# Second batch's first stage over eight slots at two groups each, three quarters of its copies on VectorE

## Chip, cores, metric

One core of one Trainium2 chip. The metric is the device time of one execution in microseconds (us), median of the runs given. The granted clock is the share of TensorE's full clock that the profile shows as let through. Engines: TensorE (PE, its weight loads PEld), VectorE (DVE), ScalarE (ACT), GpSimd (POOL).

## The reference, cut

```python
# x: (8, 3008, 256) fp32; filt_r, filt_i: (1505, 256); w_in: (256, 2048); w_out: (2048, 256)
X = np.fft.rfft(x, axis=1)
y = np.fft.irfft(X * (filt_r + 1j * filt_i)[None], n=3008, axis=1)      # filter along the sequence
h = y.reshape(24064, 256) @ w_in
out = np.maximum(0.01 * h, h) @ w_out                                   # leaky ReLU between two products
```

## The kernel before: the parts that matter

The Fourier transform of each batch is done in stages by matrix products: a first stage (`s1`, 16 groups of two matmuls), transposes (`t1`), spectral products (`s2`, `sa`, 12 groups each), transposes (`t2`), an inverse stage (`sb`, 16 groups). The feed-forward part ("moe") runs in chunks of 512 tokens. After batch 0, everything is laid out in slots: each slot has one feed-forward group of four matmuls, the Fourier tasks of a later batch, and, from slot 8 on, eight matmuls of the second product.

```python
wide   = [psp.tile([P, 2 * CH], FP32, name=f"ph{i}") for i in range(2)]   # two double banks: feed-forward
single = [psp.tile([P, CH], FP32, name=f"pf{i}") for i in range(3)]       # three single banks: Fourier stages
# ...
def s1_group(b, g, copy=nc.scalar.copy):
    def go():
        ps = bank("pf", 2, D)
        for j in range(2):
            n2 = 2 * g + j
            nc.tensor.matmul(ps[:, j, :], f1_sb[:N1, n2, :], x_sb[:N1, n2, :], start=True, stop=True)
        spread(big[(4 * b) % 3], 2 * g, ps, copy)          # the copy out of the bank: L187 in the profile
    return go
# ...
def plan(b, s1, per, t1, s2, step, lag, t2, sb):
    for g in range(16):
        at(s1 + g // per, s1_group(b, g, dve if b == 1 and g % 2 else act))
    if b + 1 < B:
        at(s1 + 15 // per, lambda: x_load(b + 1))
    for i in range(4):
        at(t1 + i, t1_part(b, i))
    for g in range(12):
        at(s2 + (step * g) // 4, s2_group(b, g))
        at(s2 + lag + (step * g) // 4, sa_group(b, g))
    for i in range(4):
        at(t2 + i, t2_part(b, i))
    for g in range(16):
        at(sb + g // 2, sb_group(b, g, dve))               # inverse, copied out by VectorE: L246

# batch, first slot of s1, its groups a slot, first slot of t1, of s2,
# slots per four groups of s2, lag of sa behind s2, first slot of t2, of sb
plan(1, 0, 3, 6, 12, 4, 3, 26, 31)
for b in range(2, B):
    z = 47 * (b - 1) - 8
    plan(b, z, 2, z + 9, z + 13, 5, 3, z + 32, z + 37)

for slot in range(SL * (NCHUNK + 1)):
    ci, g = divmod(slot, SL)
    if ci < NCHUNK:
        moe1_group(ci, g)              # matmuls L376, then the activation on ScalarE, L381
    for f in tasks.get(slot, ()):
        f()
    if ci > 0:
        moe2_slice(ci - 1, g)          # matmuls L390; every second slot ScalarE copies the result out, L397
```

Of the kernel before, what the change touches and what calls it, by code (L numbers as in the profile page):

```python
# [65 lines left out]
def kernel(  # L66
# [50 lines left out]
    def bank(kind, n, w):  # L117
        of = wide if kind == "ph" else single
        t = of[turn[kind] % len(of)]
        turn[kind] += 1  # L120
        return t[:, : n * w].rearrange("p (n w) -> p n w", n=n)
# [7 lines left out]
    def x_load(b, n0=0, nn=N2, d0=0, dn=D):  # L129

        for lo, cnt in ((0, R1),) if b + 1 < B else ((0, 64), (64, N1 - 64)):
            nc.gpsimd.dma_start(  # L132
                x_sb[lo : lo + cnt, ds(n0, nn), ds(d0, dn)],
                bass.AP(tensor=x.tensor, offset=x.offset + (b * N + lo * N2 + n0) * D + d0,
                        ap=[[N2 * D, cnt], [D, nn], [1, dn]]))
# [35 lines left out]
# [5 lines that stand above are left out]
                nc.tensor.matmul(ps[:, j, :], f1_sb[:N1, n2, :], x_sb[:N1, n2, :],  # L176
                                 start=True, stop=True)
            spread(big[(4 * b) % 3], 2 * g, ps, copy)
        return go
# [5 lines left out]
    def spread(dst, n0, ps, copy, e0=0):  # L185
        nn, de = ps.shape[1], ps.shape[2] // 2
        copy(paired(dst)[:, ds(n0, nn), ds(e0, de)], ps.rearrange("p n (e t) -> p n e t", t=2))  # L187
# [3 lines left out]
    def t1_part(b, i, flat=False):  # L191
        def go():
            a = big[(4 * b) % 3][:].bitcast(FP32)[:, ts(i, E4 * Q)].rearrange("p (e n) -> p e n", n=Q)
            o = big[(4 * b + 1) % 3][:].bitcast(FP32)
            if flat:
                o = o[:, ts(i, E4 * Q)].rearrange("p (e n) -> p e n", n=Q)
            else:
                o = o.rearrange("p (n e) -> p e n", n=Q)[:, ts(i, E4), :]
            nc.vector.transpose(o, a)  # L199
        return go  # L200


    def t2_part(b, i):
        def go():
            a = big[(4 * b + 2) % 3][:].bitcast(FP32)[:, ts(i, E4 * Q)].rearrange("p (e n) -> p e n", n=Q)
            o = big[(4 * b + 3) % 3][:].bitcast(FP32).rearrange("p (h n e) -> p h e n", h=2, n=Q)
            nc.vector.transpose(o[:, i // 2, ts(i % 2, E4), :], a)  # L207
        return go
# [3 lines left out]
    def s2_group(b, g):  # L212
        def go():
            ps = bank("pf", 2, D)
            src = big[(4 * b + 1) % 3][:].rearrange("p (n d) -> p n d", n=Q)
            nc.tensor.matmul(ps, fwd2, src[:, ds(2 * g, 2), :], start=True, stop=True)  # L216
            fa, fb = fa_sb[:, ds(2 * g, 2), :], fb_sb[:, ds(2 * g, 2), :]
            p1 = scrp.tile([P, 2, D], FP32, tag="p1", name=f"p1_b{b}_g{g}")
            p2 = scrp.tile([P, 2, D], FP32, tag="p2", name=f"p2_b{b}_g{g}")
            nc.vector.tensor_tensor(p1[:], ps, fa, AL.mult)  # L220
            nc.vector.tensor_tensor(p2[0:64], ps[64:P], fb[64:P], AL.mult)  # L221
            nc.vector.tensor_tensor(p2[64:P], ps[0:64], fb[0:64], AL.mult)  # L222
            y1 = ypp.tile([P, 2, D], FP16, tag="y", name=f"y_b{b}_g{g}")
            nc.gpsimd.tensor_tensor(y1[:], p1[:], p2[:], AL.add)  # L224
            ys[(b, g)] = y1
        return go

    def sa_group(b, g):
        def go():
            ps = bank("pf", 2, D)  # L230
            nc.tensor.matmul(ps, inv2, ys.pop((b, g))[:], start=True, stop=True)  # L231
            spread(big[(4 * b + 2) % 3], 2 * g, ps, nc.scalar.copy)
        return go

    def sb_group(b, g, copy):
        dt, h = g // 8, g % 8

        def go():
            src = big[(4 * b + 3) % 3][:].rearrange("p (h n d) -> p h n d", h=2, n=Q)
            ps = bank("pf", 4, N1)  # L240
            for j in range(4):
                n2 = 4 * h + j
                nc.tensor.matmul(ps[:, j, :], src[:, dt, n2, :], i1_sb[:, n2, :],  # L243
                                 start=True, stop=True)
            yv = yts[b % 2][:, dt, :].rearrange("p (a c) -> p a c", c=N2)
            copy(yv[:, :, ds(4 * h, 4)], ps.rearrange("p c a -> p a c"))  # L246
        return go
# [3 lines left out]
    act, dve = nc.scalar.copy, nc.vector.tensor_copy  # L251
# [70 lines left out]
    g = 0  # L322
    for n0, nn in first_parts:
        while nn:
            n = 2 if nn % 4 or n0 >= N2 - 4 else 4
            first_s1(n0, n, two[n // 4], (dve, act)[g % 2])
            n0, nn, g = n0 + n, nn - n, g + 1
# [79 lines left out]
    def at(slot, f):  # L407
        tasks.setdefault(slot, []).append(f)

    def plan(b, s1, per, t1, s2, step, lag, t2, sb):  # L410
        for g in range(16):
            at(s1 + g // per, s1_group(b, g, dve if b == 1 and g % 2 else act))
        if b + 1 < B:
            at(s1 + 15 // per, lambda: x_load(b + 1))
        for i in range(4):
# [6 lines that stand above are left out]
        for g in range(16):  # L422
            at(sb + g // 2, sb_group(b, g, dve))

    plan(1, 0, 3, 6, 12, 4, 3, 26, 31)
    for b in range(2, B):
        z = 47 * (b - 1) - 8
        plan(b, z, 2, z + 9, z + 13, 5, 3, z + 32, z + 37)

    for slot in range(SL * (NCHUNK + 1)):  # L430
        ci, g = divmod(slot, SL)
# [36 lines left out]
```

## Time and profile before

| | before |
|---|---|
| time, first three runs | 783.71 us (783.41 to 784.31) |
| span of the trace, granted clock | 783.3 us, 1.000 |
| TensorE / ScalarE / VectorE busy | 99% / 71% / 47% |
| first first-stage matmul of batch 1 | 43.85 us |
| from there to slot 8's feed-forward group | 10.96 us |
| from slot 8's group to the start of the last 64 matmuls of the second product (one line of the timeline) | 717.81 us |

Matmul records overlap: a group of four is recorded with 1.03 us and the next matmul starts 0.87 us after it began, because the profile models the end. So all TensorE intervals here are from start to start. The two ends of the 10.96 us in the timeline, batch 1's first first-stage matmul and the group that follows slot 8's feed-forward group (which starts at 54.81, 0.86 us earlier):

```profile
43.85 0.82 PE L176 MATMUL pf<-x_sb,f_sb 94*128 94x256 f16 x6
...
55.67 1.04 PE L390 MATMUL po_ps<-w_out_sb,gt_c 128*128 128x256 f16 x8
```

### The profile page before, as it was taken

The page shows a single profiled execution, that of the slowest core. Times are in us where ns is not written, and L with a number is a line of the kernel's source. Part 1 is how long each engine was busy: PE and PEld are TensorE (multiplying, and loading weights), DVE is VectorE, ACT ScalarE, POOL GpSimd, SP SyncE. Part 2 cuts the span into 40 slices and gives each one's busy share as a digit, 9 for nine tenths or more (in the row PEclk, how much of TensorE's full clock was granted, in tenths as well). Part 3 has the DMA queues.
Part 4 walks back from the last instruction along what each step waited for, and adds up shares of the span by engine and source line. Part 5 has one row for each costly group of instructions (what it writes and reads, how often), then busy time and mean ns, then how long its engine had stood idle before and what let it go on. Part 6 is the DMA issues. An engine that isn't in the chain of part 4 may idle for free.

```text
span 783.3 us, 13680 instructions
## 1 busy us (share of the span) xinstructions
PE 773.6 (99%) x5844; PEld 531.3 (68%) x5844; DVE 364.6 (47%) x458; ACT 553.2 (71%) x788; POOL 151.7 (19%) x126
## 2 busy tenths in 40 slices
PE   8899999999999999999999999999999999999998
PEld 4356677666776677766777667776677666676666
DVE  3868751875237641477306754088432765200000
ACT  3686759776686767777687775967768776666664
POOL 5974300250003300052001510025000340000000
PEclk9999999999999999999999999999999999999999
DMA  9972102301041101510105101140101001101111
GB/s 174 228 115 67 41 28 51 98 28 42 28 95 55 41 28 41 107 40 30 42 28 113 36 29 40 42 107 28 41 28 41 29 28 41 41 31 37 41 41 55
DMA packets 39388, 44.17 MB, mean 56 GB/s; under 512 B 11266, under 2 KB 37506, under 8 KB 38658
## 3 DMA queue, kind: packets, MB, share of 16 engines
q0 software_dynamic: 13136, 17.78, 13.3%
q1 hardware_dynamic: 26192, 25.53, 9.3%
q8 instruction: 45, 0.74, 0.4%
q14 instruction: 15, 0.12, 0.1%
HBM read 35.67 MB, written 24.64 MB: 77 GB/s over the span
## 4 chain that ended last, share of the span: by engine, by line
PE 93%; ACT 2%; DMA 1%; issue 1%; POOL 1%; DVE 1%; ACTq 0%; POOLq 0%
PE po_ps L390 41%; PE ph L376 41%; PE pf L176 3%; PE pf L243 2%; PE pf L216 2%; PE pf L231 2%; DMA x_sb<-in_x_dram 1%; ACT big L187 1%; PE pf L390 1%; POOL fy_h_c L276 1%; ACT gt_c L381 1%; PE ph L265 0%; PE po_ps L318 0%; DVE big L297 0%; DVE big L199 0%
## 5 line engine op out<-in xcount | busy, mean ns | idle before, releaser
L381 ACT ACTIVATE gt_c<-ph 128x1024 f16<-128x1024 f32 x376 | 385.1, 1025 | 194.6 <-PE ph L376 193.6
L376 PE MATMUL ph<-yt,w_in_sb 128*128 128x512 f16 (+7 forms) x1728 | 386.6, 351 | 0.4 <-ACT gt_c L381 0.2
L390 PE MATMUL po_ps<-w_out_sb,gt_c 128*128 128x256 f16 x2944 | 381.4, 272 | 0.6 <-ACT ost_c_t L397 0.6
L390 PEld LDWEIGHTS <-gt_c 128*128 128x128 f16 x3008 | 290.7, 98 | 86.7 <-issue 1.7
L376 PEld LDWEIGHTS <-w_in_sb 128*128 128x128 f16 x1728 | 163.0, 98 | 95.2 <-issue 1.1
L224 POOL TENSOR_TENSOR y_b_g<-p_b_g,p_b_g 128x512 f16<-128x512 f32 x84 | 106.9, 1273 | 225.8 <-DVE p_b_g L222 225.8
L199 DVE STREAM_TRANSPOSE big<-big 128x1024 f32<-128x1024 f32 x32 | 55.8, 1844 | 127.1 <-ACT big L187 127.0
L187 ACT CAST big<-pf 128x512 f16<-128x512 f32 x190 | 108.9, 605 | 2.2 <-PE pf L256 2.2
L246 DVE CAST yt<-pf 128x376 f16<-128x376 f32 x112 | 56.3, 544 | 85.9 <-PE pf L243 85.9
L220 DVE TENSOR_TENSOR p_b_g<-pf,fa_sb 128x512 f32<-128x512 f32 x84 | 58.1, 692 | 38.9 <-PE pf L216 36.3
L397 ACT COPY ost_c_t<-po_ps 128x256 f32<-128x256 f32 x184 | 69.3, 377 | 6.6 <-PE po_ps L390 5.5
L207 DVE STREAM_TRANSPOSE big<-big 128x1024 f32<-128x1024 f32 x28 | 51.1, 1940 | 34.1 <-ACT big L187 34.1
L221 DVE TENSOR_TENSOR p_b_g<-pf,fb_sb 64x512 f32<-64x512 f32 x84 | 58.2, 692 | 1.1
L222 DVE TENSOR_TENSOR p_b_g<-pf,fb_sb 64x512 f32<-64x512 f32 x84 | 57.4, 683 | 1.1
L132 POOL DMA_DIRECT2D x_sb<-in_x_dram x12 | 6.6, 553 | 253.8 <-PE pf L176 253.0
L243 PEld LDWEIGHTS <-big 128*128 128x128 f16 x448 | 25.6, 98 | 13.2
L176 PE MATMUL pf<-x_sb,f_sb 94*128 94x256 f16 x224 | 33.8, 272 | 0.1
L216 PE MATMUL pf<-big,small_sb 128*128 128x512 f16 x84 | 31.8, 379 | 0.0
L231 PE MATMUL pf<-y_b_g,small_sb 128*128 128x512 f16 x84 | 31.8, 379 | 0.0
L243 PE MATMUL pf<-i_sb,big 128*128 128x94 f16 x448 | 28.7, 206 | 0.0
L176 PEld LDWEIGHTS <-f_sb 94*128 94x128 f16 x224 | 21.0, 97 | 9.5 <-issue 1.3
L318 PE MATMUL po_ps<-idle 128*128 128x512 f16 x72 | 18.9, 406 | 1.2 <-DVE one L165 1.2
(46 smaller groups left out, 155.3 us busy)
## 6 DMA issues: line engine op xcount, KB each, us to landing
out_dram<-ost_c_t SPq DMA_DIRECT2D x92, 256.0 KB, 2.1
x_sb<-in_x_dram POOLq DMA_DIRECT2D x6, 1536.0 KB, 10.9
x_sb<-in_x_dram POOLq DMA_DIRECT2D x3, 480.0 KB, 9.8
fa_sb<-in_filt_r_dram POOLq DMA_DIRECT2D x6, 192.0 KB, 10.0
fb_sb<-in_filt_i_dram POOLq DMA_DIRECT2D x6, 192.0 KB, 8.5
w_in_sb<-in_moe_w_in_dram POOLq DMA_DIRECT2D x1, 1024.0 KB, 13.0
w_out_sb<-in_moe_w_out_dram POOLq DMA_DIRECT2D x1, 1024.0 KB, 12.7
x_sb<-in_x_dram POOLq DMA_DIRECT2D x1, 1024.0 KB, 8.1
```

What stands on the lines that cost most here:

```text
L176: nc.tensor.matmul(ps[:, j, :], f1_sb[:N1, n2, :], x_sb[:N1, n2, :], start=True, stop=True)
L187: copy(paired(dst)[:, ds(n0, nn), ds(e0, de)], ps.rearrange("p n (e t) -> p n e t", t=2))
L220: nc.vector.tensor_tensor(p1[:], ps, fa, AL.mult)
L221: nc.vector.tensor_tensor(p2[0:64], ps[64:P], fb[64:P], AL.mult)
L222: nc.vector.tensor_tensor(p2[64:P], ps[0:64], fb[0:64], AL.mult)
L224: nc.gpsimd.tensor_tensor(y1[:], p1[:], p2[:], AL.add)
L243: nc.tensor.matmul(ps[:, j, :], src[:, dt, n2, :], i1_sb[:, n2, :], start=True, stop=True)
L246: copy(yv[:, :, ds(4 * h, 4)], ps.rearrange("p c a -> p a c"))
L376: nc.tensor.matmul(ph[:, j, ds(o, ln)], w_in_sb[:, dt, ts(ct, P)], yts[b % 2][:, dt, ds(lo, ln)], start=(dt == 0), stop=(dt == NDT - 1),)
L381: nc.scalar.activation(gts[ci][:, ds(2 * g, 2), :], ph, AF.Lrelu)
L390: nc.tensor.matmul(po, gts[ci][:, ct, ts(tj, P)], w_out_sb[:, ct, :], start=(ct == 0), stop=(ct == NCT - 1))
L397: nc.scalar.copy(ost[:, tj % 2, :], po)
```

## The change

Intent: in slots 0 to 7 ScalarE has both the activations and half of the first-stage copies of batch 1. Spreading the groups and giving VectorE twelve of the sixteen copies should let TensorE set the pace. The later stages of batch 1 move by a slot.

```diff
-            at(s1 + g // per, s1_group(b, g, dve if b == 1 and g % 2 else act))
+            at(s1 + g // per, s1_group(b, g, dve if b == 1 and g % 4 < 3 else act))
...
-    plan(1, 0, 3, 6, 12, 4, 3, 26, 31)
+    plan(1, 0, 2, 8, 13, 4, 3, 27, 32)
```

## The prediction

> **What bounds the kernel now.** I read the page first (busy shares, then the chain that ended last), then the waits, then the timeline of the stretch that the change touches. The busy shares and the chain:
>
> ```profile
> PE 773.6 (99%) x5844; PEld 531.3 (68%) x5844; DVE 364.6 (47%) x458; ACT 553.2 (71%) x788; POOL 151.7 (19%) x126
> PE 93%; ACT 2%; DMA 1%; issue 1%; POOL 1%; DVE 1%; ACTq 0%; POOLq 0%
> ```
>
> TensorE is 93% of the chain. A busy TensorE can still hide gaps, so I checked the pace: from the start of one four-matmul group to the next instruction group the timeline shows 0.87 us (0.217 us for each 512 columns) and 0.44 us for four first-stage matmuls of 256 columns (0.11 us each), everywhere after 55 us. There the same work takes the same time however it is ordered, so no reordering gains anything. A gain can only come from a stretch where TensorE is not at that pace. The chain in order of time shows where the other engines enter it:
>
> ```profile
> 42.60 0.56 DVE yt L309
> 45.94 1.05 ACT gt_c L381
> ...
> 49.33 1.07 ACT gt_c L381
> ...
> 51.74 1.15 ACT big L187 x2
> 52.89 0.94 ACT gt_c L381
> ...
> 53.87 1.97 PE ph L376 x8
> ```
>
> From 44 to 53.9 us the chain runs through ScalarE; then TensorE takes it over. This is exactly slots 0 to 7 of the second phase, where the second batch's first stage is packed three groups to a slot. The timeline of TensorE and ScalarE there, with durations whose modelled matmul ends overlap (so I use starts only):
>
> ```profile
> 48.03 1.03 PE L376 MATMUL ph<-yt,w_in_sb 128*128 128x512 f16 x4
> 48.32 1.16 ACT L187 CAST big<-pf 128x512 f16<-128x512 f32 x2
> 49.33 1.07 ACT L381 ACTIVATE gt_c<-ph 128x1024 f16<-128x1024 f32 x1
> 49.75 1.03 PE L376 MATMUL ph<-yt,w_in_sb 128*128 128x512 f16 x4
> 50.24 0.71 ACT L187 CAST big<-pf 128x512 f16<-128x512 f32 x1
> 51.44 1.03 PE L376 MATMUL ph<-yt,w_in_sb 128*128 128x512 f16 x4
> ...
> 52.67 1.03 PE L376 MATMUL ph<-yt,w_in_sb 128*128 128x512 f16 x4
> 53.87 1.97 PE L376 MATMUL ph<-yt,w_in_sb 128*128 128x512 f16 x8 [0.17 <-ACT gt_c L381]
> ```
>
> Two slots take 51.44 - 48.03 = 3.41 us. TensorE needs for them 2 x 0.87 + 6 x 0.22 = 3.06 us; ScalarE has two activations and three copies and is busy without a gap (10.71 us of the 10.96 between 43.85 and 54.81 by the windows view). So ScalarE paces the stretch, and TensorE loses about 0.17 us a slot, plus some at 52.7 to 53.9, where the last activations drain.
>
> The second place that matters is where batch 1 ends and batch 2 begins, at slots 38 and 39:
>
> ```profile
> 115.38 0.51 PE L243 MATMUL pf<-i_sb,big 128*128 128x94 f16 x8
> 115.74 1.03 PE L390 MATMUL po_ps<-w_out_sb,gt_c 128*128 128x256 f16 x8
> 115.76 1.01 DVE L246 CAST yt<-pf 128x376 f16<-128x376 f32 x2 [1.08 <-PE pf L243]
> 116.61 1.03 PE L376 MATMUL ph<-yt,w_in_sb 128*128 128x512 f16 x4
> 117.47 0.60 PE L176 MATMUL pf<-x_sb,f_sb 94*128 94x256 f16 x4
> ```
>
> The last inverse groups (L243) run in slot 38, VectorE takes their banks from 115.76 to 116.77, and batch 2's first stage (L176) starts a slot later, after its banks are free. Nothing waits.
>
> [...] VectorE's copies record 0.69 us and follow one another at 0.60, ScalarE's record 0.605 in the mean, and the activation 1.025. So moving a copy to VectorE makes it a little slower, not free. [...] Here the first stage, the spectral stages and the inverse all rotate through the same three single banks, and the activations' matmuls through two double ones. [...] the matmul at 53.87 starts 0.04 us after the activation that emptied its bank.
>
> **The change, part by part.** Nothing is removed; all counts of matmuls, copies and transfers stay.
>
> 1. *Sixteen groups over eight slots at two each.* TensorE then needs 0.87 + 0.44 = 1.30 us a slot.
> 2. *Twelve of sixteen copies on VectorE (eight before).* ScalarE has, per two slots, two activations and one copy. At the spacing seen (an activation and the next start 0.92 apart, a copy 0.55) that is about 2 x 0.95 + 0.55 = 2.45 us against 2.61 for TensorE. VectorE has three copies: 3 x 0.65 = 1.95 us. So TensorE becomes the slowest, by 0.16 us per two slots.
> 3. *Do the bank rotations keep up?* A double bank is filled in 0.87, picked up 0.2 us later, held 1.02 and released: about 2.1 us after its first matmul, and needed again 2.61 after it. Where a copy sits ahead of the activation on ScalarE the margin falls to about 0.25 us. A single bank is needed again three groups later, 1.5 slots or 1.52 us at the nearest; a VectorE copy of the second group of a slot, queued behind the first, is done about 1.55 us after its matmuls start against 2.4 needed in that phase. All margins are positive but none is large.
> 4. *The sum for the first stretch.* The first activation group still waits for the yt copy ending at 43.15, so the first stage still starts at 43.85. Between there and the ninth group (start of slot 8) lie 7 x 0.867 + 16 x 0.218 = 9.56 us at full pace, so slot 8 starts at 53.41. Before, the x8 entry at 53.87 holds two groups; the second, slot 8's, starts 54.81 in the trace (the next group follows at 55.67). Gain: 54.81 - 53.41 = 1.40 us.
> 5. *The later stages move by one slot.* The transposes need all sixteen copies; the last is now ScalarE's, behind slot 7's activation, done at about 52.1 + 2.6 = 54.7. The four take 7.28 us (53.74 to 61.02 before), so end near 62.0. The first spectral matmul stands in slot 13, at 53.41 + 5 x 1.735 + 0.87 = 62.95. It has 0.9 us to spare. The other intervals (5 slots from transpose to spectral, 14 to the second transpose, 5 to the inverse) are as before or shorter by that one slot, and the input load that follows the first stage has over 40 us before it is read. No cost.
> 6. *The new collision.* Batch 1's inverse now ends in slot 39, where batch 2's first stage begins. The order of instructions in the built kernel confirms it: the two inverse groups, then two first-stage groups in the same slot. That is four uses of three single banks in a row, and the fourth waits for the copy of the first. By the offsets of slot 38 above, that copy ends 0.38 + 0.53 = 0.91 us after the first inverse matmul starts, and TensorE wants the bank at 0.36 + 0.22 = 0.58. Stall: about 0.35 to 0.4 us with the release. The last inverse copy ends at 1.39, while slot 40's group, which is the first to read batch 1's result, starts after 0.36 + 0.22 + 0.38 + 0.22 + 0.87 = 2.05 us, so this does not wait.
>
> Net: -1.40 + 0.38 = -1.02 us, 783.71 to 782.69, say 782.7 us (0.13%).
>
> **Rivals.** First, *no collision cost*: if VectorE released the bank sooner the result would be 782.3. The offsets of eight such slots in the trace are the same within 0.02 us, which speaks against it. Second, *the freed time turns into bank waits*: at 0.16 us per two slots ScalarE is nearly as slow as TensorE, and an activation that starts late by a copy costs TensorE at the next double bank; with two or three such waits of 0.2 us the gain shrinks to 0.9 and the time is 783.2. For it speaks that part of the copies in this stretch are longer (0.71 us when both engines copy). Third, *the delay of one slot hurts*: if slot 40's first read of the batch waits for the last inverse copy, or the transposes overrun slot 13, up to 0.9 us comes back and the time is about 783.6. The slack above, 0.66 and 0.9 us, speaks against it. Fourth, *ScalarE alone was the bound and its relief is worth more*: four copies of 0.55 are 2.2 us, which would give 781.5 before the collision; against it, TensorE's own full pace caps the gain at 1.40.
>
> **Range and chances.** The four cases lie between 781.5 and 783.6, the middle ones between 782.3 and 783.2. The three runs of before spread over 0.9 us, with one of them 0.6 above the median, so I widen to 781.9 to 783.7. A change of 2% is 15.7 us; the whole stretch is 11 us long, so faster by 2% is out of reach and slower by 2% would need a stall that repeats in every batch, while batches 2 to 7 are untouched: 0.5% each, 99% within.
>
> **What would show it.** Right: slot starts 1.30 us apart from 43.85 on and slot 8's group near 53.4; ScalarE no longer without gaps there; the transposes from about 54.7 to 62.0 without a wait of the first spectral matmul; near slot 39 (about 115.3 us in the new trace) a gap of 0.35 to 0.4 us ahead of a first-stage matmul, put down to the inverse copy on VectorE; everything later earlier by 1.0 us. Wrong: slots 1.4 us or longer with waits for the activation; no gap at slot 39, or a second one at slot 40.

The sum comes to -1.40 + 0.38 = -1.02 us, 783.71 to 782.69, and the 0.867 and 0.218 us in its first term are the 0.87 us (four matmuls of 512 columns) and 0.44 us (two first-stage groups) of the trace of the kernel before.

## The result

| | before | changed |
|---|---|---|
| time, six runs each, two sessions | 784.36 us (783.41 to 784.82) | 783.44 us (782.80 to 784.70) |
| ratio | | 0.9992 (95%: 0.9979 to 1.0004) |
| span of the trace | 783.3 us | 782.1 us |
| first first-stage matmul of batch 1 | 43.85 us | 43.62 us |
| from there to slot 8's group | 10.96 us | 9.56 us |
| from slot 8's group to the last 64 matmuls | 717.81 us | 718.30 us |

A ratio is the mean time of one kernel's fast runs over that of the other's of the same rounds, so it is not quite the ratio of the medians. By medians the change saves 0.92 us, by the ratio about 0.63; against the first three runs of the kernel before (783.71) the changed kernel is only 0.27 us faster. The interval of the ratio reaches from 1.65 us faster to 0.31 us slower, so these twelve times alone don't show a gain, and that their medians come so near to what the traces show is luck.

The chain of waits of the changed kernel in slots 0 to 8 (start, us, what). Where the chain before went through ScalarE's activations and copies, it is now TensorE alone:

```profile
43.78 0.44 PE pf L176 x4
...
53.35 0.86 PE ph L376 x4
```

The two ends of the first interval and two slots between them in its timeline (start, us, engine, line, operation, output and input; in brackets the idle time before it and who ended it):

```profile
43.62 0.60 PE L176 MATMUL pf<-x_sb,f_sb 94*128 94x256 f16 x4
...
47.97 1.03 PE L376 MATMUL ph<-yt,w_in_sb 128*128 128x512 f16 x4
...
49.26 2.06 DVE L187 CAST big<-pf 128x512 f16<-128x512 f32 x3 [0.54 <-PE pf L176]
...
50.34 1.02 ACT L381 ACTIVATE gt_c<-ph 128x1024 f16<-128x1024 f32 x1 [0.18 <-PE ph L376]
50.58 1.03 PE L376 MATMUL ph<-yt,w_in_sb 128*128 128x512 f16 x4
...
53.18 1.03 PE L376 MATMUL ph<-yt,w_in_sb 128*128 128x512 f16 x4
```

Slot 8's group starts at 53.18, 9.56 us after 43.62. Two slots take 50.58 - 47.97 = 2.61 us, and ScalarE and VectorE now wait for TensorE, not the other way round. The timeline at slot 39:

```profile
115.58 0.51 PE L243 MATMUL pf<-i_sb,big 128*128 128x94 f16 x8
115.93 0.38 PE L176 MATMUL pf<-x_sb,f_sb 94*128 94x256 f16 x2
115.95 1.00 DVE L246 CAST yt<-pf 128x376 f16<-128x376 f32 x2 [1.08 <-PE pf L243]
116.56 0.38 PE L176 MATMUL pf<-x_sb,f_sb 94*128 94x256 f16 x2 [0.24 <-DVE yt L246]
```

The second first-stage group starts 0.63 us after the first instead of 0.22: it waits 0.41 us for the bank that the inverse group of the same slot filled. (The bracket says 0.24, because idle time is counted from the modelled end of the matmul before, 0.16 us later than the next could have started.) The transposes, VectorE's row of four, end in time for the first spectral matmul:

```profile
54.49 7.29 DVE L199 STREAM_TRANSPOSE big<-big 128x1024 f32<-128x1024 f32 x4 [0.56 <-ACT big L187]
62.73 0.38 PE L216 MATMUL pf<-big,small_sb 128*128 128x512 f16 x1
```

They end at 61.78, the spectral matmul starts unhindered at 62.73.

So the mechanism came out as predicted, but for 0.09 us that are traced below. What did not fit was the number measured by time. The theory (A) was: the change is worth what the trace shows, 0.9 to 1.0 us, and the rest is a spread of the start of the kernel, which the change doesn't touch. The rival (B): the trace overstates it, and the timed gain is 0.3 to 0.6 us.

### The profile page after: what moved, and what is told of

It reads as the page before. It is cut to its first block, busy times and chain, and to the rows that moved or that the text cites. A ratio compares the mean times of both kernels' runs of the same rounds, so it can differ in the third digit from the quotient of the medians.

```text
span 782.1 us, 13672 instructions
## 1 busy us (share of the span) xinstructions
PE 773.4 (99%) x5844; PEld 531.4 (68%) x5844; DVE 367.3 (47%) x462; ACT 551.2 (70%) x784; POOL 152.3 (19%) x126
## 4 chain that ended last, share of the span: by engine, by line
PE 94%; DMA 2%; POOL 2%; ACT 1%; DVE 1%; issue 1%; POOLq 0%
PE ph L376 41%; PE po_ps L390 41%; PE pf L176 3%; PE pf L243 2%; PE pf L231 2%; PE pf L216 2%; DMA fb_sb<-in_filt_i_dram 2%; PE pf L390 1%; POOL fy_h_c L276 1%; ACT big L187 0%; POOL x_sb L132 0%; DVE big L297 0%; ACT big L290 0%; POOL fb_sb L140 0%; ACT gt_c L381 0%
## 5 line engine op out<-in xcount | busy, mean ns | idle before, releaser
L187 ACT CAST big<-pf 128x512 f16<-128x512 f32 x186 | 106.6, 604 | 1.7 <-PE pf L256 1.7
L397 ACT COPY ost_c_t<-po_ps 128x256 f32<-128x256 f32 x184 | 69.4, 377 | 6.6 <-PE po_ps L390 5.4
```

What stands on the lines that cost most here:

```text
L187: copy(paired(dst)[:, ds(n0, nn), ds(e0, de)], ps.rearrange("p n (e t) -> p n e t", t=2))
L397: nc.scalar.copy(ost[:, tj % 2, :], po)
```

## Experiments

All kernels computed the right result. The table collects what the traces gave; the runs follow one by one. S is the start of batch 1's first first-stage matmul; the code ahead of S is the same in the first ten.

| kernel | S | S to slot 8 | slot 8 to the last 64 matmuls | time, median (runs) |
|---|---|---|---|---|
| before | 43.85 | 10.96 | 717.81 | 784.36 (6) |
| before again | 43.33 | 10.98 | 717.81 | 784.52 (5) |
| changed | 43.62 | 9.56 | 718.30 | 783.44 (6) |
| changed again | 43.53 | 9.56 | 718.30 | 783.46 (5) |
| no overlap | 42.78 | 9.56 | 717.90 | 783.08 (5) |
| best | 43.17 | 9.56 | 716.89 | 782.55 (5) |
| spread only | 42.76 | 10.69 | 718.29 | one run |
| split only | 44.39 | 10.71 | 717.81 | one run |
| all on VectorE | 42.80 | 9.56 | 718.30 | one run |
| two overlaps | 43.42 | 9.56 | 719.06 | one run |
| before / changed, 60 warming matmuls | 48.58 / 49.68 | 10.97 / 9.56 | 717.80 / 718.29 | 790.52 / 789.92 (5) |
| before / changed, gate at 23 us | 58.67 / 59.69 | 10.96 / 9.56 | 717.82 / 718.30 | 800.13 (5) / 799.05 (4) |
| before / changed, gate at 17 us | 50.19 / 50.19 | 10.98 / 9.56 | 717.84 / 718.31 | 791.22 / 790.24 (5) |

### The kernel before, again (before_again)

No edit.

> The kernel before, unchanged, timed against itself, to see what a run varies by and where. Theory A (the variation lies in the start, before the first first-stage matmul of batch 1 at 43.85 us; all after it is fixed): from that matmul to slot 8's group 10.96 us and from slot 8's group to the end 728.5 us, each within 0.1 us of the first trace, while the start differs by some tenths of a microsecond; ratio of times 1.000 within 0.001. Theory B (the stretches in the middle vary too, so that gaps of 0.4 us in a trace say nothing): one of the two intervals differs by over 0.3 us.

Measured: ratio 0.9996 (0.9984 to 1.0009); the two intervals 10.98 and 717.81 us, within 0.02 us of the first trace; S 0.52 us earlier. The middle is fixed, the start is not: over the ten traces whose code ahead of S is the same, S lies between 42.76 and 44.39 us. That is 1.6 us, more than the whole change.

### The changed kernel, again (after_again)

No edit.

> The changed kernel again. Theory A (the change saves 1.40 us before slot 8 and gives back 0.4 us at slot 39, whatever the run): first first-stage matmul to slot 8 9.56 us, slot 8 to the end 728.9 us, the ratio of times 0.9987 within 0.001. Theory B (the saving in the single trace was luck): the first interval is over 9.8 us.

Measured: 9.56 and 718.30 us, as in the first trace of it; 783.46 us against 784.32 for the kernel before in the same rounds, ratio 0.9989 (0.9977 to 1.0002). The saving of 1.40 us and the loss near slot 39 are not luck.

### The overlap at slot 39 taken away (no_overlap)

```diff
-    plan(1, 0, 2, 8, 13, 4, 3, 27, 32)
+    plan(1, 0, 2, 8, 13, 4, 3, 27, 31)
```

> The changed kernel with batch 1's inverse groups one slot earlier (from slot 31), so that they end before batch 2's first stage starts. Theory A (the gap at slot 39 is the bank wait behind the inverse copy): no gap at slots 38 to 40, slot 8 to the end 728.5 us as in the kernel before, first interval still 9.56; ratio of times 0.998. Theory B (the 0.4 us come from the shift by a slot as such, or the inverse now waits for the second transposes): slot 8 to the end stays at 728.9 or more, with a gap near slot 31 or 39.

Measured: no wait of a first-stage matmul; from slot 8 on 717.90 us against 718.30 in the changed kernel, so 0.40 us back. The list of TensorE's waits from 42 us on has the line that the changed kernel's has, and no longer its second, for the bank:

```profile
PE po_ps L390 <- ACT ost_c_t L397: 0.5, 3, 0.2
```

(The columns are us in total, times, longest.) The changed kernel's list:

```profile
PE po_ps L390 <- ACT ost_c_t L397: 0.6, 3, 0.2
PE pf L176 <- DVE yt L246: 0.2, 1, 0.2
```

Ratio 0.9983 (0.9970 to 0.9997). The loss was the bank wait of the overlap, not the shift by a slot. The shift has a cost too, but a small one: the 0.09 us that stay over the kernel before are in the traces at slot 28. In the kernel before, the feed-forward group there starts at 94.72 us and the second product's matmuls at 95.59, 0.87 later; in the changed kernel 93.10 and 94.05, in the one without overlap 92.26 and 93.21, both 0.95. Moved from slot 26 to 27, the last copy of `sa` now stands on ScalarE ahead of slot 27's output copy (L397), and the matmuls start 0.06 us after that copy ends (93.99 in the changed kernel). That is read from the traces; no run was made for it. The kernel before has the same 0.08 us at three later batches (271.97, 458.77 and 645.58 us). The list shows none of them, because the end of a TensorE record is modelled 0.16 us late (1.03 us for four matmuls, 0.87 from start to start).

### Two slots of overlap (two_overlaps)

```diff
-        plan(b, z, 2, z + 9, z + 13, 5, 3, z + 32, z + 37)
+        plan(b, z - (b == 2), 2, z + 9, z + 13, 5, 3, z + 32, z + 37)
```

(on the changed kernel)

> The changed kernel with batch 2's first stage one slot earlier (from slot 38), so that two slots hold inverse and first-stage groups together. Theory A (each such slot costs one wait for the bank of an inverse copy, 0.4 us): two gaps of 0.4 us ahead of a first-stage matmul, slot 8 to the end 729.3 us against 728.9 in the changed kernel. Theory B (the gap of the changed kernel belongs to slot 39's place, not to the overlap): one gap, 728.9 us.

Measured: two waits of the same kind, each again 0.63 us from start to start, but 719.06 us, 0.76 above the changed kernel instead of 0.41. The rest is a third wait, 0.36 us, which nobody expected:

```profile
113.65 0.38 PE L176 MATMUL pf<-x_sb,f_sb 94*128 94x256 f16 x2
114.28 0.38 PE L176 MATMUL pf<-x_sb,f_sb 94*128 94x256 f16 x2 [0.24 <-DVE yt L246]
...
116.58 0.38 PE L176 MATMUL pf<-x_sb,f_sb 94*128 94x256 f16 x2
117.21 0.38 PE L176 MATMUL pf<-x_sb,f_sb 94*128 94x256 f16 x2 [0.24 <-DVE yt L246]
```

```profile
131.42 1.04 PE L376 MATMUL ph<-yt,w_in_sb 128*128 128x448 f16 x8
132.65 0.60 PE L390 MATMUL po_ps<-w_out_sb,gt_c 128*128 128x256 f16 x4 [0.19 <-ACT ost_c_t L397]
```

It is the same wait for ScalarE's output copy that all kernels so far but this one have at three batches only. Those three have their first stage starting in an even slot (86, 180, 274), and moving batch 2 from slot 39 to 38 gave it the wait too. ScalarE copies an output out in every second slot, so an eight-slot stretch that starts on an even slot ends on one with such a copy while ScalarE is behind. That the parity decides is what these four cases say; no run was made for it alone.

### The best version: those three waits as well (best)

```diff
-            at(s1 + g // per, s1_group(b, g, dve if b == 1 and g % 4 < 3 else act))
+            at(s1 + g // per, s1_group(b, g, dve if (g % 4 < 3 if b == 1 else g % 4 == 3) else act))
```

(on the version without overlap)

> As the run without overlap, and in batches 2 to 7 every fourth first-stage copy moved from ScalarE to VectorE, which is idle in those slots. Theory A (ScalarE falls behind in those stretches, and the three waits for its output copy of 0.2 us, at the end of three of the stretches, are all that it costs): slot 8 to the end 727.9 us, those waits gone; ratio of times 0.997. Theory B (TensorE never really loses there): 728.5 us as without it.

Measured: the list of TensorE's waits from 45 us on is empty; slot 8 to the last 64 matmuls 716.89 us, 1.01 less than without overlap. I expected 0.6, from 0.2 us in the list for each of three waits. From start to start each is 0.35 us, which gives 1.05: the list understates a wait of TensorE by the 0.16 us that its records are too long. Ratio to the kernel before 0.9973 (0.9961 to 0.9986), 782.55 against 784.32 us: the fastest kernel here, and next to the version without overlap the only one of the plain kernels whose interval excludes 1.

### Each half of the change alone (spread_only, split_only)

```diff
-            at(s1 + g // per, s1_group(b, g, dve if b == 1 and g % 4 < 3 else act))
+            at(s1 + g // per, s1_group(b, g, dve if b == 1 and g % 2 else act))
```

(on the changed kernel: two groups to a slot, copies shared evenly)

> Two groups to a slot and the later stages as in the changed kernel, but every second copy on each engine as before. The time from the first first-stage matmul of batch 1 to slot 8's group is 10.96 us before and 9.56 us changed. Theory A (ScalarE's load sets the pace once it is above TensorE's): ScalarE needs two activations of 0.88 to 0.92 and two copies of 0.55 per two slots, 2.86 to 2.94 us, against TensorE's 2.61; so the interval is about 10.4 us and most slots wait for an activation. Theory B (the spreading alone does it): 9.56 to 9.7 us.

```diff
-            at(s1 + g // per, s1_group(b, g, dve if b == 1 and g % 2 else act))
+            at(s1 + g // per, s1_group(b, g, dve if b == 1 and g % 4 < 3 else act))
```

(on the kernel before: three groups to a slot, three quarters of the copies on VectorE)

> Three groups to a slot and the later stages as before, but three quarters of the copies on VectorE. Theory A (besides ScalarE's load there is a second loss: slots 6 and 7 hold nothing but the activation group, and two double banks allow one such group per 1.07 us at best, where TensorE needs 0.87): the interval to slot 8 is about 10.0 to 10.2 us, with waits for the activation in slots 6 to 8 and few before. Theory B (the split alone does it): 9.56 to 9.7 us.

Measured: 10.69 and 10.71 us, against 10.96 with neither and 9.56 with both. Each alone gives a quarter of a microsecond, both 1.40. In the first, ScalarE takes one activation and one copy a slot and sets the pace, 1.45 us a slot (the pace, 2.90 us for two slots, is as expected; my 10.4 was added up too low, since seven slots at 0.145 us over TensorE's 1.305 already make 10.57, and the second slot loses 0.25):

```profile
46.20 1.03 PE L376 MATMUL ph<-yt,w_in_sb 128*128 128x512 f16 x4
46.74 0.65 ACT L187 CAST big<-pf 128x512 f16<-128x512 f32 x1
...
47.65 1.03 PE L376 MATMUL ph<-yt,w_in_sb 128*128 128x512 f16 x4
```

In the second, ScalarE is relieved but two other waits take over, larger than the 0.4 to 0.6 us I had given the second of them:

```profile
44.81 3.08 DVE L187 CAST big<-pf 128x512 f16<-128x512 f32 x5 [1.12 <-PE pf L176]
46.75 0.38 PE L176 MATMUL pf<-x_sb,f_sb 94*128 94x256 f16 x2 [0.22 <-DVE big L187]
...
55.10 1.02 PE L376 MATMUL ph<-yt,w_in_sb 128*128 128x512 f16 x4 [0.39 <-ACT gt_c L381]
```

VectorE's row of five copies keeps the single banks too long (the group at 46.75 starts 0.40 us late from start to start, after the third of these copies), and slots 6 and 7, with nothing between their activation groups, run into the two double banks (0.73 us at slot 8). Spreading cures both, but only if ScalarE is fast enough to follow. The 1.07 us a group in the expectation is an estimate from the trace of the kernel before: a double bank is filled in 0.87 us, picked up 0.2 later, held 1.02 by the activation and written again 0.04 after it, 2.13 us for two groups.

### All sixteen copies on VectorE (all_vector)

```diff
-            at(s1 + g // per, s1_group(b, g, dve if b == 1 and g % 4 < 3 else act))
+            at(s1 + g // per, s1_group(b, g, dve if b == 1 else act))
```

> The changed kernel with all sixteen copies on VectorE. Per two slots VectorE has four copies at 0.60 to 0.68 us, 2.4 to 2.7 us, against TensorE's 2.61. Theory A (the bound is whichever engine is slowest, so the split has a flat optimum): the interval to slot 8 is 9.56 to 9.8 us. Theory B (VectorE's queue and the three single banks make TensorE wait in most slots): over 10 us.

Measured: 9.56 us again. VectorE works without a gap, sixteen copies in 10.41 us, 0.65 from start to start, which is just TensorE's 1.30 us for two:

```profile
43.22 10.41 DVE L187 CAST big<-pf 128x512 f16<-128x512 f32 x16 [1.12 <-PE pf L176]
```

The share of three quarters is thus on a flat optimum: twelve and sixteen give the same, eight does not.

### Where the spread comes from, first try (before_late, after_late)

```diff
-    keep_warm(28)
+    keep_warm(60)
```

(the zero matmuls ahead of the first data, on both kernels)

> The kernel before with 60 warming matmuls instead of 28 ahead of everything, about 6.9 us more, so that the first loads have landed when TensorE reaches their data. Theory A (the run-to-run spread of 1 to 2 us comes from the loads of the first 37 us): the five times lie within 0.5 us of each other, about 790 us. Theory B (the spread comes from elsewhere: launch, the end, the clock): they spread over 1.2 us or more as without it. The interval from the first first-stage matmul of batch 1 to slot 8 stays 10.97 us.

> The changed kernel with the same 60 warming matmuls, on the same chip. Theory A: its five times lie within 0.5 us, and their median is 0.95 us (1.40 less 0.45) below that of the kernel before with 60, now clear of the spread. Theory B (the traces mislead and the timed gain is smaller, as the 0.27 us between the changed kernel's median and the first three runs of the kernel before): the medians differ by under 0.5 us.

Measured: 790.52 (789.75 to 791.28) and 789.92 us (789.48 to 790.32). The spread stayed 1.5 and 0.8 us, the medians differ by 0.60: a miss, the loads are not the whole of it. But S was 48.58 in one trace and 49.68 in the other, and the two timelines of weight loads show why. Before:

```profile
3.73 0.15 PEld L318 LDWEIGHTS <-idle 128*128 128x128 f16 x1 [0.28 <-issue]
4.13 11.11 PEld L318 LDWEIGHTS <-idle 128*128 128x128 f16 x52 [0.25 <-issue]
```

Changed:

```profile
5.87 0.15 PEld L318 LDWEIGHTS <-idle 128*128 128x128 f16 x1 [0.28 <-issue]
6.29 10.04 PEld L318 LDWEIGHTS <-idle 128*128 128x128 f16 x47 [0.28 <-issue]
```

The single entries are warming matmuls at 0.43 us each, the merged ones at 0.22. TensorE doubles its pace at 4.13 us in one run and at 6.29 in the other. Half of 2.16 us is 1.08, and both the first data matmul (15.57 and 16.67) and S are 1.10 us apart. Over the twelve traces up to here the change of pace lies between 4.13 and 6.29 us. The first warming matmul starts at 1.20 us in every trace, so the earliest change comes 2.93 us after it and the latest of the twelve 5.09 us after it. The halved pace and the varying moment are in the lines above; what sets the moment, no run here shows.

### A gate that came too late (before_gated, after_gated)

```diff
+    for _ in range(17):
+        nc.vector.memset(big[2][:].rearrange("p (e n t) -> p e n t", n=Q, t=2)[:, :, NC:Q, :], 0.0)
+    nc.vector.memset(single[0][:], 0.0)
```

(on the kernels with 60 warming matmuls, after the first clear of `big[2]`: VectorE holds the first bank until a fixed time)

> The kernel before with 60 warming matmuls, and the first bank that the real data go into held by VectorE with a fixed row of 19 clears until about 18.2 us, later than the slowest warming seen (16.7 us) and than the first loads. Theory A (what is left of the spread with 60 warming matmuls is the moment at which TensorE changes from 0.43 to 0.22 us a matmul, 4.1 us in one trace and 6.3 in the other, which moves everything after it by up to 1.1 us): the first first-stage matmul of batch 1 stands near 51.3 us, and the five times lie within 0.5 us, about 792.5 us. Theory B (the spread comes after the start or outside the trace): they still spread over 1 us.

> The changed kernel with the same gate. Theory A: its first first-stage matmul of batch 1 stands within 0.1 us of that of the gated kernel before, the five times lie within 0.5 us, and their median is 0.95 us (0.8 to 1.1) below. Theory B: the medians differ by 0.3 to 0.6 us, as those of the runs with 60 warming matmuls do, and the traces overstate the gain.

Measured: 800.13 (799.63 to 800.52) and 799.05 us (798.25 to 799.73, four fast runs), granted clock 0.996 and 0.993. My estimate of the gate was off: each clear is recorded with 0.91 us but waits for the one before, 1.19 from start to start, so the gate opened at 23.16 us. TensorE had been idle for 6.0 us (before) and 6.6 us (changed) and had lost its pace: eight first-stage matmuls took 1.7 us instead of 0.87 from start to start, and it found its pace again at different moments (S 58.67 and 59.69). The medians are 1.08 us apart, but this is the old spread in another place, so the run is inconclusive. It does show that a gate takes up the varying moment: the pace changed at 7.09 us in one trace and at 5.79 in the other, and the first data matmul starts at 23.16 in both.

### The gate in time (before_gated12, after_gated12)

```diff
-    for _ in range(17):
+    for _ in range(12):
```

> As the gated kernel before, with 12 clears instead of 17, so that the gate opens at about 17.4 us, at most 1.9 us after the last warming matmul. Theory A (the moment of TensorE's change of pace is the spread): the pace is kept, the first first-stage matmul of batch 1 stands near 50.4 us, the five times lie within 0.5 us, about 791.6 us. Theory B: they spread over 1 us or more.

> The changed kernel with the same gate. Theory A: its first first-stage matmul of batch 1 within 0.1 us of the other's, the five times within 0.5 us, the medians 0.95 us apart (0.8 to 1.1). Theory B: medians 0.3 to 0.6 us apart, or a spread of 1 us.

Measured: before 791.13, 791.14, 791.22, 791.27, 791.28; changed 790.23, 790.23, 790.24, 790.27, 790.33. The five times spread over 0.15 and 0.10 us, where those of the kernels without the gate spread over 0.8 to 2.1 (five to nine runs each), and the medians are 0.98 us apart, the means 0.95. The same first data matmul stands in both traces (lines are three lower, because of the three lines added):

```profile
17.20 0.38 PE L259 MATMUL pf<-x_sb,f_sb 94*128 94x256 f16 x2 [0.69 <-DVE pf L171]
```

and changed:

```profile
17.20 0.38 PE L259 MATMUL pf<-x_sb,f_sb 94*128 94x256 f16 x2 [0.70 <-DVE pf L171]
```

S is 50.19 us in both. (The pace changed at 5.77 and 5.76 us, so this pair of traces alone wouldn't show what the gate does; the narrow spread of the five times does.) So the time saved is what the traces said, and theory B is out: with the start held, a gain of 0.12% shows in five runs. The gate waits out both TensorE's change of pace and the first loads; no run takes one of them away alone from the plain kernels. But their ten traces speak for the loads. S doesn't follow the change of pace: with all copies on VectorE the pace changes at 6.29 us, the latest of the ten, and S is 42.80; in the first trace of the kernel before it changes at 4.59, and S is 43.85. From the first data matmul to S it takes 33.02 to 34.67 us, where both traces with 60 warming matmuls take 33.01. And in nine of the ten the chain of waits runs through a first load of `x_sb` or of the filters (`x_sb` for 11.02 us in the first trace of the kernel before, `fb_sb` for 14.48 in that of the changed one); only with all copies on VectorE, where it takes the 33.02 us, does it run through the 28 warming matmuls.

## Why the prediction was right or wrong

The steps about the mechanism, in the order of the prediction:

- *No reordering gains anything after 55 us.* Wrong, though the change doesn't rest on it: three waits of 0.35 us for ScalarE's output copy stood there, and moving copies took them away (the best version, 1.01 us less from slot 8 on).
- *TensorE sets the pace (steps 1 to 3).* Right. 1.30 us a slot, no wait for a bank or an activation in eight slots. The second rival, that small margins turn into waits, did not occur.
- *Slot 8's group 1.40 us earlier (step 4).* Right: S to slot 8 predicted 9.56, measured 9.56 in every trace of the changed kernel.
- *Transposes and spectral products still meet (step 5).* Right: predicted end near 62.0 and 0.9 us to spare, measured 61.78 and 0.95. But "no cost" of moving the later stages by a slot was not exact: it cost 0.09 us at slot 28.
- *The bank wait at slot 39 (step 6).* Right in place and cause, 0.41 us for a predicted 0.35 to 0.4; the whole part after slot 8 grew by 0.49, of which 0.09 are slot 28's. The other rivals are out: the collision had its cost, which went only where the overlap went; slot 40 and the first spectral matmul did not wait; and relieving ScalarE was worth 1.40 us, not 2.2.
- *The net of -1.02 us.* -0.91 in the traces (-1.40 + 0.49), -0.98 by the medians of the gated pair.

The step that failed is the first term of the sum, "783.71 to 782.69": the level from which the change was subtracted. Three runs of one session were taken for it, though the start moves by 1.6 us from run to run. With six runs the kernel before is 784.36, and in the later rounds its median was between 784.3 and 784.9. The level was mis-sized by 0.65 us, two thirds of the effect. So 783.44 was measured for 782.69, 0.75 us above: 0.65 of it is the level, 0.10 the change itself (0.92 by the medians for 1.02). Against the three runs only 0.27 us of the gain are left. The prediction widened its range by the spread of the three runs and gave no cause for the spread; with a chain of waits that begins with 11.02 us of one load, and warming matmuls at two paces, the profile of before showed where to look. What sets the level of a single run is shown in part only: the change of pace with 60 warming matmuls, the loads in the plain kernels by their traces alone.

## What to carry to other kernels

When a stretch is held by several things at once (here ScalarE's load, the single banks and the double banks), removing one may give little: two changes worth 0.27 and 0.25 us alone were worth 1.40 together. When moving a stage, look at what it now overlaps at its far end: one slot shared by two stages that rotate through three banks gave back 0.41 us, and moving the stage a slot earlier took that away. For effects below a part in a thousand, compare intervals inside the traces from start to start, or hold the start of the kernel fixed; the medians of five free runs cannot tell 0.3 from 1.0 us here.
